# A hybrid attention and gated-layer kernel: the third token tile loaded and transposed earlier, around the value projections of the first tiles

## The chip, the cores and the metric

The kernel runs on one core of one Trainium2 chip. The metric is the device time of one execution in microseconds (us). The five engines of the core run side by side and meet at semaphores: PE (TensorE: matmuls and transposes; its weight loads are shown as PEld), DVE (VectorE), ACT (ScalarE), POOL (GpSimd) and SP (SyncE, which issues the DMAs).

## What is computed

`x` has 2048 tokens of 512 numbers, in bf16. It is normalised once and goes through two branches whose results are added to it:

```
xn  = layernorm(x)
qkv = xn @ wqkv                                  # 32 heads of 16
phi_q, phi_k = softmax(+-(q @ w_phi)), softmax(+-(k @ w_phi))   # joined, 32 features
kv, z = sum over tokens of phi_k * v, of phi_k
o   = (phi_q @ kv) / (phi_q . z + 1e-6)
out = x + o @ wo + ((xn @ w_gate) * (xn @ w_up)) @ w_down       # 1792 hidden columns
```

## The kernel before

The 2048 tokens are 16 tiles of 128 rows. A tile must be layer-normed and transposed (`xnT`, the contraction dimension on the partitions) before PE can multiply it with a weight. For tiles 4 to 15 this runs beside PE's other work, and DMA does the transposing. For tiles 0 to 3, at the start, it is done on the spot, and this is the part that the change touches:

- `centre(n)` (lines 174 to 180): on DVE, the statistics of tile n (`bn_stats` at L156, `bn_aggr` at L157) and the subtraction of the mean (L177, gives `xn`); then two small POOL instructions (L161, L162) that give the row scale `rst`.
- `lt(n)` (lines 213 to 222): PE transposes the four 128-column blocks of `xn` into one PSUM bank (L219), and ACT copies them to `xnT` in two halves (L222).
- `proj(ps, n, wv, js)` (L251): up to four matmuls of 512 columns, the value projection v of tile n, one for each 128-row block j of `wv`. Block j needs the j-th part of `xnT` of that tile, and the half of `wv` that holds it: blocks 0 and 1 lie in the first half, 2 and 3 in the second.
- `vcopy(n, ps, eng)` (lines 338 to 345): v, scaled by `rst`, from PSUM to SBUF, on ACT (L343) or DVE (L345).
- `half(w, ...)` (L285): four matmuls that make one 128-column block of gate or up, here for the first 256 tokens only (tiles 0 and 1); `gate_copy` (L291, ACT) and `hidden` (L297, DVE) take it out of PSUM.

The schedule is written by hand (`manual_schedule`): each engine executes its instructions in the order in which the program text issues them, and an instruction that waits holds up all that follow it on its engine. So the lines 349 to 377 are the order of each of the engines at the start. Before the real work PE runs nine matmuls on constants (`warm_up`, L334), whose result is not used.

All loads are issued by SP on one queue, in the order of lines 84 to 101. The sixteen DMA engines share out each load. A DMA's landing here means that all its parts have arrived.

PSUM has eight banks. In the first part two of them hold `pv[0]` and `pv[1]`; the other six (`bank()`) go round: each new tile takes the bank that was given out six calls earlier, and waits for that one's last reader.

After these lines the program is one long row of gate and up matmuls, k, v and q projections, sums over tokens, and in the end the output projections (`fin`, L315 and L318).

Of the kernel before, what the change touches and what calls it, by code (L numbers as in the profile page):

```python
# [21 lines left out]
def kernel(  # L22
# [12 lines left out]
    nc = tc.nc  # L35
# [6 lines left out]
    DC = D // P  # L42
# [21 lines left out]
    wv = wpool.tile([P, DC, D], BF16)  # L64
# [9 lines left out]
    def dma_x(lo, hi):  # L74
        nc.sync.dma_start(out=xall[:, lo:hi, :], in_=x_view(lo, hi))

    def dma_cols(eng, w, src, lo, hi, at=0):
        eng.dma_start(out=w[:, :, lo - at:hi - at], in_=src[:, lo:hi].rearrange("(c p) f -> p c f", p=P))
# [7 lines left out]
    for lo in (0, 2):  # L86
        nc.sync.dma_start(out=wv[:, lo:lo + 2, :],
                          in_=A_wqkv[lo * P:(lo + 2) * P, 2 * D:3 * D].rearrange("(c p) f -> p c f", p=P))
    dma_x(2, 3)
    dma_cols(nc.sync, wg, B_w_gate, 0, 2 * P)  # L90
    dma_x(3, 4)
    dma_cols(nc.sync, wu, B_w_up, 0, 2 * P)
# [56 lines left out]
    def bank(name, dt=F32, n=TT):  # L149
        return ps_s.tile([P, n], dt, name=name, tag="s")  # L150
# [3 lines left out]
    def ln_stats(n, mv):  # L154
        stats = lnpool.tile([P, nc.vector.BN_STATS_DIM], F32, name="stats")
        nc.vector.bn_stats(out=stats[:], in_=xall[:, n, :])  # L156
        nc.vector.bn_aggr(out=mv, in_=stats[:])  # L157

    def ln_rstd(mv, k, rstd):
        ve = lnpool.tile([P, GT], F32, name="ve")  # L160
        nc.gpsimd.tensor_scalar(out=ve[:, 0:k], in0=mv[:, 0:k, 1], scalar1=EPS, scalar2=None, op0=ALU.add)  # L161
        nc.gpsimd.tensor_tensor(out=rstd, in0=ve[:, 0:k], in1=mhalf[:, 0:k], op=ALU.pow)  # L162
# [11 lines left out]
    def centre(n):  # L174
        ln_stats(n, mv0[:, n, :])
        xn = xnpool.tile([P, D], BF16, name="xn")
        nc.vector.tensor_scalar(out=xn[:], in0=xall[:, n, :], scalar1=mv0[:, n, 0:1], scalar2=None,  # L177
                                op0=ALU.subtract)
        ln_rstd(mv0[:, n:n + 1, :], 1, rst[:, n:n + 1])
        xns[n] = xn  # L180
# [32 lines left out]
    def lt(n, nbanks=1):  # L213
        step = DC // nbanks
        tps = []
        for lo in range(0, DC, step):
            tp = bank("tp", BF16).rearrange("p (c t) -> p c t", c=DC)
            for c in range(lo, lo + step):
                nc.tensor.transpose(out=tp[:, c, :], in_=xns[n][:, c * P:(c + 1) * P], identity=ident[:])  # L219
            tps.append(tp)  # L220
        for lo in range(0, DC, 2):
            nc.scalar.copy(out=xnT[:, lo:lo + 2, n * P:(n + 1) * P], in_=tps[lo // step][:, lo:lo + 2, :])  # L222
# [3 lines left out]
    def make_bd():  # L226
        bo, wp = BO[:], wphi[:]
        nc.vector.tensor_tensor(out=bd[:], in0=_bcast_ap(bo, [bo.ap[0], [0, DC], [E1, 8], [1, DH]]),
                                in1=_bcast_ap(wp, [wp.ap[0], [DH, DC], [0, 8], [1, DH]]), op=ALU.mult)
# [19 lines left out]
    def proj(ps, n, w, js=range(DC)):  # L249
        for j in js:  # L250
            nc.tensor.matmul(ps, lhsT=xnT[:, j, n * P:(n + 1) * P], rhs=w[:, j, :],  # L251
                             start=(j == 0), stop=(j == DC - 1))
# [29 lines left out]
    def half(w, name, T, f, lo, hi):  # L282
        ps = bank(name)[:, 0:hi - lo]
        for c in range(DC):
            nc.tensor.matmul(ps, lhsT=w[:, c, f * P:(f + 1) * P], rhs=xnT[:, c, T * TT + lo:T * TT + hi],  # L285
                             start=(c == 0), stop=(c == DC - 1))
        return ps

    def gate_copy(ps, n):
        g_sb = gpool.tile([P, TT], BF16, name="g_sb")  # L290
        nc.scalar.copy(out=g_sb[:, 0:n], in_=ps)  # L291
        return g_sb

    def hidden(T, f, ps, g_sb, lo, hi):
        if T not in hTs:
            hTs[T] = hpool.tile([P, FC, TT], BF16, name="hT", tag="h")
        nc.vector.tensor_tensor(out=hTs[T][:, f, lo:hi], in0=ps, in1=g_sb[:, 0:hi - lo], op=ALU.mult)  # L297
# [34 lines left out]
    def warm_up(k, n=TT):  # L332
        for _ in range(k):
            nc.tensor.matmul(warm[:, 0:n], lhsT=ones[:, 0:P], rhs=ones[:, 0:n], start=True, stop=True)  # L334
# [3 lines left out]
    def vcopy(n, ps, eng=nc.scalar):  # L338
        dst, src = vts[n % NV][:, :, :, 0:DH], ps.rearrange("p (a b c) -> p a b c", a=8, b=4)
        if n >= GT:  # L340
            nc.scalar.copy(out=dst, in_=src)  # L341
        elif eng is nc.scalar:
            nc.scalar.activation(out=dst, in_=src, func=AF.Identity, scale=rst[:, n:n + 1])  # L343
        else:
            eng.tensor_scalar(out=dst, in0=src, scalar1=rst[:, n:n + 1], scalar2=None, op0=ALU.mult)  # L345

    with tc.tile_pool(name="ps_v", bufs=1, space=PSUM) as ps_v:
        pv = [ps_v.tile([P, D], F32, name=f"pv{n}") for n in range(2)]
        centre(0)
        centre(1)  # L350
        lt(0, nbanks=2)
        warm_up(1)
        proj(pv[0][:], 0, wv, range(1))
        lt(1)
        proj(pv[0][:], 0, wv, range(1, DC))
        proj(pv[1][:], 1, wv)
        centre(2)
        vcopy(0, pv[0])
        lt(2)
        g = [half(wg, "g", 0, f, 0, 2 * P) for f in range(2)]  # L360
        g_sb = [gate_copy(ps, 2 * P) for ps in g]
        centre(3)
        vcopy(1, pv[1], nc.vector)
        pv2 = bank("pv")
        proj(pv2, 2, wv, range(2))
        lt(3)
        proj(pv2, 2, wv, range(2, DC))
        vcopy(2, pv2, nc.vector)
        for f in range(2):
            hidden(0, f, half(wu, "u", 0, f, 0, 2 * P), g_sb[f], 0, 2 * P)  # L370
        pv3 = bank("pv")
        proj(pv3, 3, wv)
        vcopy(3, pv3, nc.vector)
        make_bd()
        nc.gpsimd.tensor_scalar(out=nrst[:], in0=rst[:], scalar1=-1.0, scalar2=None, op0=ALU.mult)
        nc.gpsimd.tensor_tensor(out=r2[:], in0=rst[:], in1=rst[:], op=ALU.mult)
        nc.gpsimd.tensor_tensor(out=M4[:], in0=BO[:, 0:4, :], in1=BO[:, 4:8, :], op=ALU.add)
# [138 lines left out]
```

## Time and profile before

| | us |
|---|---|
| median of three runs | 221.6 (221.21 to 221.74) |
| the profiled execution: its time | 221.94 |
| the profiled execution: its span | 220.2 |
| PE busy in the span | 214.7 (97%) |
| DVE busy | 140.3 (64%) |
| ACT busy | 87.5 (40%) |
| POOL busy | 73.0 (33%) |

The span is what the profile shows from the first instruction to the last; 1.7 us of the execution's time lie around it. The granted TensorE clock is shown as 1.00. Matmuls are pipelined: the duration of one runs on into the next, so the step from one start to the next is what a matmul costs PE. A row "0.59 ... x2" with 379 ns for one says that the second started 0.21 us after the first.

### The profile page before, as it was taken

The page shows a single profiled execution, that of the slowest core. Times are in us where ns is not written, and L with a number is a line of the kernel's source. Part 1 is how long each engine was busy: PE and PEld are TensorE (multiplying, and loading weights), DVE is VectorE, ACT ScalarE, POOL GpSimd, SP SyncE. Part 2 cuts the span into 40 slices and gives each one's busy share as a digit, 9 for nine tenths or more (in the row PEclk, how much of TensorE's full clock was granted, in tenths as well). Part 3 has the DMA queues.
Part 4 walks back from the last instruction along what each step waited for, and adds up shares of the span by engine and source line. Part 5 has one row for each costly group of instructions (what it writes and reads, how often), then busy time and mean ns, then how long its engine had stood idle before and what let it go on. Part 6 is the DMA issues. An engine that isn't in the chain of part 4 may idle for free.

```text
span 220.2 us, 3493 instructions
## 1 busy us (share of the span) xinstructions
PE 214.7 (97%) x1283; PEld 104.8 (48%) x1307; DVE 140.3 (64%) x239; ACT 87.5 (40%) x161; POOL 73.0 (33%) x64
## 2 busy tenths in 40 slices
PE   8999999999999999999999999999999999999994
PEld 3564445444444444444454444444444444454443
DVE  5667976886598766657499874197655745454321
ACT  3525587458654775464444221231322322100000
POOL 5500556363338573635135433033033033000000
PEclk9999999999999999999999999999999999999999
DMA  6999995402202241202008345214431431412401
GB/s 186 235 310 385 367 224 75 87 0 51 48 0 48 51 72 25 48 3 46 4 18 130 71 95 116 55 24 95 95 74 24 95 71 28 93 50 71 72 26 48
DMA packets 47249, 19.91 MB, mean 90 GB/s; under 512 B 37504, under 2 KB 46976, under 8 KB 47104
## 3 DMA queue, kind: packets, MB, share of 16 engines
q1 hardware_dynamic: 47232, 19.69, 37.8%
q8 instruction: 10, 0.16, 0.3%
q14 instruction: 7, 0.06, 0.1%
HBM read 8.67 MB, written 2.10 MB: 49 GB/s over the span
## 4 chain that ended last, share of the span: by engine, by line
PE 88%; DVE 3%; DMA 2%; issue 2%; ACT 1%; POOL 1%; SPq 1%; DVEq 0%; ACTq 0%
PE fin L315 22%; PE g L285 20%; PE u L285 20%; PE fin L318 6%; PE q L251 6%; PE k L251 5%; PE pv L251 5%; DMA xall<-in_A_x_dram 2%; PE ab L458 2%; PE kv L397 2%; DVE sums L266 1%; DVE stats L156 1%; ACT e L262 1%; DVE rs L268 1%; POOL rstd L162 0%
## 5 line engine op out<-in xcount | busy, mean ns | idle before, releaser
L285 PE MATMUL g<-xnT,wg 128*128 128x512 bf16 (+1 forms) x227 | 57.2, 371 | 0.4
L285 PE MATMUL u<-xnT,wu 128*128 128x512 bf16 (+1 forms) x231 | 57.5, 372 | 0.1
L297 DVE TENSOR_TENSOR hT<-u,g_sb 128x512 bf16<-128x512 f32 (+1 forms) x58 | 37.1, 648 | 24.2 <-PE u L285 15.4
L291 ACT CAST g_sb<-g 128x512 bf16<-128x512 f32 (+1 forms) x58 | 33.3, 575 | 48.2 <-PE g L285 48.1
L266 DVE TENSOR_REDUCE sums<-e 128x64 f32<-128x1024 f32 x32 | 38.9, 1216 | 20.5 <-ACT e L262 20.5
L270 POOL TENSOR_TENSOR phiq<-e,rs 128x1024 bf16<-128x1024 f32 x16 | 30.9, 1933 | 62.9 <-DVE rs L268 54.1
L315 PE MATMUL fin<-wd,hT 128*128 128x512 bf16 (+2 forms) x231 | 50.3, 366 | 0.3
L270 POOL TENSOR_TENSOR phik<-e,rs 128x1024 bf16<-128x1024 f32 x16 | 30.9, 1932 | 44.5 <-DVE rs L268 32.3
L285 PEld LDWEIGHTS <-wu 128*128 128x128 bf16 x232 | 22.7, 98 | 25.9
L315 PEld LDWEIGHTS <-hT 128*128 128x128 bf16 x238 | 22.5, 98 | 24.7
L285 PEld LDWEIGHTS <-wg 128*128 128x128 bf16 x232 | 22.0, 98 | 23.4
L251 PEld LDWEIGHTS <-xnT 128*128 128x128 bf16 x192 | 17.5, 98 | 17.8 <-ACT xnT L222 0.6
L251 PE MATMUL pv<-wv,xnT 128*128 128x512 bf16 x62 | 22.1, 386 | 0.2
L326 DVE TENSOR_TENSOR o_sb<-fin,xall 128x512 bf16<-128x512 f32 (+2 forms) x13 | 8.4, 650 | 20.5 <-PE fin L318 19.7
L251 PE MATMUL k<-W1k,xnT 128*128 128x512 bf16 x61 | 20.7, 379 | 0.0
L268 DVE RECIPROCAL rs<-sums 128x64 f32<-128x64 f32 x32 | 17.7, 553 | 3.1
L318 PE MATMUL fin<-wo,oT 128*128 128x512 bf16 (+2 forms) x66 | 16.3, 366 | 0.1
L251 PE MATMUL q<-W1q,xnT 128*128 128x512 bf16 x60 | 16.0, 378 | 0.2
L260 ACT ACTIVATE e<-q 128x512 f32<-128x512 f32 x12 | 7.2, 597 | 22.2 <-PE q L251 22.2
L341 ACT CAST vt<-pv 128x512 bf16<-128x512 f32 x12 | 7.0, 587 | 16.9 <-PE pv L251 16.9
L156 DVE BATCH_NORM_STATS2 stats<-xall 128x6 f32<-128x512 bf16 x16 | 10.7, 670 | 3.0 <-DMA xall<-in_A_x_dram 2.9
L468 DVE TENSOR_TENSOR otok<-ab,rden 128x512 bf16<-128x512 f32 x16 | 11.1, 691 | 0.6
(55 smaller groups left out, 126.4 us busy)
## 6 DMA issues: line engine op xcount, KB each, us to landing
out_dram<-o_sb SPq DMA_DIRECT2D x15, 128.0 KB, 1.9
wd<-in_B_w_down_dram SPq DMA_DIRECT2D x1, 1792.0 KB, 15.5
wg<-in_B_w_gate_dram SPq DMA_DIRECT2D x2, 640.0 KB, 6.8
wu<-in_B_w_up_dram SPq DMA_DIRECT2D x2, 640.0 KB, 8.0
xall<-in_A_x_dram SPq DMA_DIRECT2D x1, 1024.0 KB, 11.9
xall<-in_A_x_dram SPq DMA_DIRECT2D x4, 128.0 KB, 3.2
wv<-in_A_wqkv_dram SPq DMA_DIRECT2D x2, 256.0 KB, 2.9
wg<-in_B_w_gate_dram SPq DMA_DIRECT2D x2, 256.0 KB, 4.8
```

The costliest lines, as they stand in the source:

```text
L156: nc.vector.bn_stats(out=stats[:], in_=xall[:, n, :])
L251: nc.tensor.matmul(ps, lhsT=xnT[:, j, n * P:(n + 1) * P], rhs=w[:, j, :], start=(j == 0), stop=(j == DC - 1))
L266: nc.vector.tensor_reduce(out=sums[:], in_=ev, axis=AX.X, op=ALU.add)
L268: nc.vector.reciprocal(out=rs[:].rearrange("p a b -> p (a b)"), in_=sums[:])
L270: nc.gpsimd.tensor_tensor(out=phi[:].rearrange("p g (x f) -> p (g x) f", f=DH), in0=ev, in1=rs[:].to_broadcast((P, 2 * H, DH)), op=ALU.mult)
L285: nc.tensor.matmul(ps, lhsT=w[:, c, f * P:(f + 1) * P], rhs=xnT[:, c, T * TT + lo:T * TT + hi], start=(c == 0), stop=(c == DC - 1))
L291: nc.scalar.copy(out=g_sb[:, 0:n], in_=ps)
L297: nc.vector.tensor_tensor(out=hTs[T][:, f, lo:hi], in0=ps, in1=g_sb[:, 0:hi - lo], op=ALU.mult)
L315: nc.tensor.matmul(ps, lhsT=hTs[T][:, f, t4 * P:(t4 + 1) * P], rhs=wd[:, f, lo:lo + w], start=(f == 0), stop=False)
L318: nc.tensor.matmul(ps, lhsT=oTs[n][:, c, :], rhs=wo[:, c, lo:lo + w], start=False, stop=(c == DC - 1))
L326: nc.vector.tensor_tensor(out=o_sb[:], in0=ps, in1=xres, op=ALU.add)
L468: nc.vector.tensor_tensor(out=o_tok[:].rearrange("p (b h d) -> p b h d", b=2, d=DH), in0=abv[:, :, :, 0:DH], in1=rden[:].to_broadcast((P, ...
```

## The change

The load of x tile 2 is issued between the two halves of `wv` instead of behind both. On PE, the transposes of tile 2 go between the second and third matmul of v of tile 1, all of v of tile 2 goes ahead of the two gate blocks, and the transposes of tile 3 go behind these blocks, in one piece with nothing of v around them. On DVE, `centre(2)` has its old place behind `centre(1)`, and one `vcopy` less is to be done: that of tile 1 goes to ACT. On ACT, the copies of `xnT` of tile 2 now precede the two `vcopy`s. No instruction is added or removed, except that v of tile 1 is scaled by an ACT instruction in place of a DVE one.

```
     for lo in (0, 2):
         nc.sync.dma_start(out=wv[:, lo:lo + 2, :],
                           in_=A_wqkv[lo * P:(lo + 2) * P, 2 * D:3 * D].rearrange("(c p) f -> p c f", p=P))
-    dma_x(2, 3)
+        if lo == 0:
+            dma_x(2, 3)
     dma_cols(nc.sync, wg, B_w_gate, 0, 2 * P)
...
         proj(pv[0][:], 0, wv, range(1, DC))
-        proj(pv[1][:], 1, wv)
         centre(2)
+        proj(pv[1][:], 1, wv, range(2))
+        lt(2)
+        proj(pv[1][:], 1, wv, range(2, DC))
         vcopy(0, pv[0])
-        lt(2)
+        vcopy(1, pv[1])
+        pv2 = bank("pv")
+        proj(pv2, 2, wv)
         g = [half(wg, "g", 0, f, 0, 2 * P) for f in range(2)]
         g_sb = [gate_copy(ps, 2 * P) for ps in g]
         centre(3)
-        vcopy(1, pv[1], nc.vector)
-        pv2 = bank("pv")
-        proj(pv2, 2, wv, range(2))
+        vcopy(2, pv2, nc.vector)
         lt(3)
-        proj(pv2, 2, wv, range(2, DC))
-        vcopy(2, pv2, nc.vector)
         for f in range(2):
             hidden(0, f, half(wu, "u", 0, f, 0, 2 * P), g_sb[f], 0, 2 * P)
         pv3 = bank("pv")
```

## The prediction

> **What bounds the kernel now.** I read the page first: PE is busy for 97% of the span and makes up 88% of the chain that ended last. Then PE's own waits, over the whole span:
>
> ```profile
> PE 214.7 (97%) x1283; PEld 104.8 (48%) x1307; DVE 140.3 (64%) x239; ACT 87.5 (40%) x161; POOL 73.0 (33%) x64
> PE 88%; DVE 3%; DMA 2%; issue 2%; ACT 1%; POOL 1%; SPq 1%; DVEq 0%; ACTq 0%
> ```
>
> ```profile
> PE warm L334 <- PEq L500: 0.8, 1, 0.8
> PE tp L219 <- DVE xn L177: 0.5, 1, 0.5
> ```
>
> Besides the start PE waits just once, in the first slices, for `xn` of tile 2. Behind that, its starts follow one another at the pace of the matmuls up to the end at 217 us. So what is won or lost on PE before about 12 us arrives at the end in full, unless another engine or a load is late by then. The chain of waits says what the one wait hangs on (start, length):
>
> ```profile
> 2.69 4.27 DMA xall<-in_A_x_dram
> 6.96 0.02 issue
> 6.98 0.70 DVE stats L156
> 7.71 0.19 DVE mv L157
> 7.90 0.02 issue
> 7.93 0.36 DVE xn L177
> 8.29 0.05 issue
> 8.34 0.40 PE tp L219 x4
> ```
>
> Tile 2 of x, issued at 2.69, lands at 6.96; DVE needs 1.31 (6.98 to 8.29), and the transposes start at 8.34. PE's timeline gives the size of the wait (start, length, in brackets the idle time):
>
> ```profile
> 5.50 0.63 PE L219 MATMUL tp<-ident,xn 128*128 128x128 bf16 x4
> 5.93 1.86 PE L251 MATMUL pv<-wv,xnT 128*128 128x512 bf16 x7
> 8.34 0.40 PE L219 MATMUL tp<-ident,xn 128*128 128x128 bf16 x4 [0.55 <-DVE xn L177]
> 8.57 1.04 PE L285 MATMUL g<-xnT,wg 128*128 128x256 bf16 x8
> ...
> 11.62 0.81 PE L251 MATMUL pv<-wv,xnT 128*128 128x512 bf16 x3
> 12.27 0.60 PE L285 MATMUL g<-xnT,wg 128*128 128x256 bf16 x4
> ```
>
> The last v matmul of tile 1 starts at 7.41 (narrow window) and costs 0.216, the step between starts, so PE could go on at 7.63. The wait is 8.34 - 7.63 = 0.71; the bracket's 0.55 counts from the modelled end. The start of the g matmuls behind v of tile 3, 12.27, is my yardstick.
>
> **Loads.** SP issues x2 at 2.18 in place of 2.69 and the second half of wv at about 2.7 in place of 2.18, each in about 0.47; all later issues keep their times. The first half of wv lands at 4.47, the second at 5.25, so 256 KB took 0.78 and a tile of x (128 KB) about 0.39. x2 then lands at 4.47 + 0.39 = 4.86 and wv's second half at 5.25 + 0.39 = 5.64. These are estimates from landings. For the other end: before, x2 landed 1.71 behind wv, not 0.39. The packet records show one 1 KB packet, begun at 5.19, of 1.34 us, where most took some 0.05; fifteen of x2's sixteen parts had landed by 5.85, the last at 6.96. Nothing says whether this packet belongs to that place in the queue, to that moment, or to this one execution.
>
> **DVE, tile 2.** DVE is free at 5.39 (`centre(1)` ends 5.04 + 0.35) and x2 is there. `centre(2)` ends at 5.40 + 1.31 = 6.71, and its transposes may start at 6.76. Its two POOL instructions move forward with it; no other work is queued there.
>
> **PE, step by step.** Up to 6.98 the order is as before: v of tile 0 needs wv's second half at 6.33 (landing 5.64), and matmuls 0 and 1 of tile 1 start at 6.76 and 6.98. Transposes at 7.195, 0.44 behind the 6.76 that they need; four at 0.056 (0.40 less 0.22 for one, over three), to 7.42. Matmuls 2 and 3 of tile 1, to 7.85. Putting transposes into an open sum I cost at nothing else: tile 1's stood so in v of tile 0, and the next row starts 0.11 behind the last of them.
>
> Now v of tile 2, which has no gate work left between it and its own transposes. Last transpose at 7.36, its length 0.22, 0.04 to ACT, the copy 0.37, 0.06 to the weight load and matmul (the steps from tile 1's rows: 5.82, 6.18, 6.55, 6.60): 8.05. PE is free at 7.85, so a **new wait** of 0.20. ACT is idle then: `vcopy(0)` now stands behind the copies. The second copy ends at 8.27, before matmul 2 needs it at 8.48. Bounds: nothing, if the copy starts half done, to 0.43, if the 0.86 from tile 0's transposes to its first v (4.24 to 5.10, matmuls still at double the step) holds, less the cover of two matmuls; the row that it is nearest to is tile 1's, so 0.20.
>
> Four matmuls to 8.91. Gates: eight at 0.109, to 9.79; `wg` landed at 7.97, so no wait. Transposes of tile 3: `xn` was ready for them at 9.75 (PEld row), DVE's order up to there is unchanged, x3 lands where it did: 9.79 to 10.01. Up: to 10.88 (`wu` landed at 9.23). v of tile 3 needs the copy of its transposes: last one at 9.95 + 0.22 + 0.04 = 10.21; ACT has by then `vcopy(0)` 8.16, `vcopy(1)` 8.74 (0.58 a step, as two 512-wide ACT rows at 20.94 and 21.52), gate copies at 9.55 and 9.99, so the copy runs from about 10.26 to 10.63, ready at 10.68, under cover of the up matmuls by 0.2. Four matmuls: yardstick at **11.75 in place of 12.27: -0.52**, that is the 0.71 gone and the 0.20 new.
>
> Edits at nothing, with their cover: `vcopy(2)` on DVE (0.75) starts behind `centre(3)` at 9.61, ends at 10.36; v of tile 3 takes that bank, the sixth later, at 10.88: 0.5 of cover. `vcopy(1)` on ACT is read by the sums at 31 us. Later loads: wu's third part lands at 17.28 and was used at 19.01; now at 18.5. Transposed tile 4 landed at 32.91 behind the last weight loads and was used at 34.36; now at 33.8, 0.9 of cover. So the gain is not given back by a load.
>
> **The sum.** 221.94 - 0.52 = 221.42, made against the profiled execution's own time, which is 0.34 above the median of 221.6. I don't subtract that 0.34 again: if part of the 0.71 was absent in the other runs, it is the very thing that made them shorter, and without it before would be 221.94 - 0.71 = 221.23, close to the lowest run, 221.21. Forecast **221.4**, that is no change that a measurement of this kernel (about 0.3%, 0.66 us) can tell.
>
> The page "TensorE: Matmul & The Clock Gate" of the Trainium skill (Part 1) says that the clock doubles at the end of a free-running window of about 3.4 us, so at another moment in each execution. Here the 512-column steps go from 0.43 to 0.22 at 6.3, while the clock is shown as 1.00 throughout. By that rule an earlier doubling would let PE reach the wait sooner: both kernels' times then spread by several tenths, in the direction of a larger gain.
>
> **Rivals.**
>
> *The tile is not late in most runs.* If x2 lands by 5.85, as fifteen of its parts did, `xn` is ready at 5.87 + 1.36 = 7.23, ahead of 7.63: before has no wait, and after still has its 0.20. For: runs 0.2 to 0.7 below the profiled one, one slow packet. Against: the profile is what there is. Time: 221.6 + 0.2 = 221.8.
>
> *The late part falls on wv (slower).* The second half of wv now stands last of the pair, with less slack: needed at 6.33, estimated 5.64. If the slow packet stays at its moment or place, that half lands at 6.96 as the pair did, and v of tile 0 waits 0.63 at its third matmul, with everything behind it. Then 221.42 + 0.63 = 222.05, slower than before by 0.1 of its profiled time and 0.45 of the median. It loses against the profiled time from a landing at 6.85 on, and by over 0.3% of the median from 7.17 on. Against: wv's halves landed in 2.8 and 3.1 us, without a laggard. The page "DMA: Bandwidth & Descriptors" of the Trainium skill ("Why a DMA increments its semaphore by 16 and not by 1") speaks for this rival: a wait ends only when the slowest of the engines has delivered. Hanging on it: x2's parts, from 5.40 to 6.96, agree.
>
> *More is won.* If PE runs ahead of the profiled pace, before waits longer for the same late tile, and the new order gains up to the whole wait and some: 221.94 - 0.71 and the profile's own 0.34 less give 220.9. For: the wait ends by a load, at a fixed time. Against: the 0.20 needs a copy that is not faster then.
>
> *The change does nothing,* because the wait moves whole to v of tile 2 or to tile 3's transposes, which have 0.04 to spare: 221.6. It takes an `xn` of tile 3 later by 0.5, which only a later x3 makes; its issue has not moved.
>
> **Chances.** Forecast 0.45, tile not late 0.2, late wv 0.15, more won 0.15, nothing 0.05. Faster by over 0.3% (below 220.94): two thirds of "more won" and a little of the forecast, 0.18. Slower by over 0.3% (above 222.26): half of "late wv", some of "tile not late", and what I haven't seen, 0.17. Within: 0.65. Range 220.85 (more won) to 222.15 (late wv).
>
> **What would show it.** Right: x2 landed near 4.9, `stats` of tile 2 at 5.4, transposes in the v row of tile 1 at 7.2, no wait for `xn`, an idle weight load of about 0.2 until ACT's copy ahead of v of tile 2, g of tiles 2 and 3 near 11.75. Wrong: a PE wait at the third v matmul of tile 0 that ends by wv, a wait ahead of tile 3's transposes, or a PE wait behind 12 us that was not there.

## The result, and the profile after

| | us |
|---|---|
| before, median of 20 runs | 221.68 (221.05 to 222.29) |
| changed, median of 20 runs | 222.03 (221.66 to 222.49) |
| ratio | 1.0017, 95% interval 1.0009 to 1.0025 |
| profiled execution after: time, span | 222.22, 220.5 |

The change costs 0.35 us. It was forecast to bring 0.2 to 0.5, so the direction was wrong; the time lies in the range, and near the 222.05 that the rival "the late part falls on wv" had worked out. That the median meets this number to 0.02 is partly luck: the rival's sum starts from a profiled execution, and the one profiled after the change took 222.22, 0.17 more than the sum (0.07 from the start of the waiting matmul, 7.03 in place of 6.96, and 0.10 from a later place, see below). PE's waits in the changed kernel (us in total, times, longest):

```profile
PE pv L252 <- DMA wv<-in_A_wqkv_dram: 0.9, 1, 0.9
PE warm L335 <- PEq L501: 0.8, 1, 0.8
PE pq L239 <- ACT g_sb L292: 0.2, 1, 0.2
```

The wait for `xn` of tile 2 is gone, and one for the second half of `wv` is there, longer than the old one. The third line, a short wait of a projection fold at 51 us, is new too. The chain of waits names the same load, in the place where x tile 2 stood before (2.69, 4.27):

```profile
2.69 4.30 DMA wv<-in_A_wqkv_dram
6.98 0.04 issue
7.03 1.02 PE pv L252 x4
```

PE's timeline after:

```profile
5.77 0.38 PE L252 MATMUL pv<-wv,xnT 128*128 128x512 bf16 x1
7.03 1.02 PE L252 MATMUL pv<-wv,xnT 128*128 128x512 bf16 x4 [0.88 <-DMA wv<-in_A_wqkv_dram]
7.89 0.39 PE L220 MATMUL tp<-ident,xn 128*128 128x128 bf16 x4
8.11 1.66 PE L252 MATMUL pv<-wv,xnT 128*128 128x512 bf16 x6
...
11.58 1.03 PE L252 MATMUL pv<-wv,xnT 128*128 128x512 bf16 x3
12.45 0.38 PE L286 MATMUL g<-xnT,wg 128*128 128x256 bf16 x2
```

The second v matmul of tile 0 frees PE at 5.99, the third starts at 7.03: 1.04 lost (the bracket's 0.88 counts from the modelled end). Everything behind runs as the prediction stepped it, 5.42 from the third matmul to the yardstick (6.33 to 11.75 in the sum), and the yardstick is 12.45 in place of 12.27. That is 0.18 of the 0.28 between the two profiled executions. The other 0.10 arises at 41.8 us, see below.

The stages from 4 to 6 us, first before, then after (the last column is GB/s moved by the DMA engines, the one ahead of it their busy share):

```profile
4.00:5.00 1.00, 1.00 (x6) 0.45 (x5) 0.96 (x3) 0.33 (x2) 0.86 (x2) 1.00 1.05 350
5.00:6.00 1.00, 1.00 (x7) 0.66 (x7) 0.35 (x2) 0.32 (x2) 0.82 (x2) 1.00 1.05 265
```

```profile
4.00:5.00 1.00, 1.00 (x6) 0.45 (x5) 0.96 (x3) 0.27 (x2) 0.91 (x2) 1.00 0.96 201
5.00:6.00 1.00, 1.00 (x7) 0.47 (x7) 0.96 (x3) 0.40 (x3) 0.77 (x2) 1.00 0.71 215
```

From 4 to 5 us the DMA engines were about as busy (0.96 against 1.05) but moved far less; from 5 to 6 us they were less busy too (0.71). The packet records say how: eight 1 KB packets that began between 4.50 and 4.71 took 0.57 to 0.81 us each, where most take about 0.05.

### The profile page after: what moved, and what is told of

It reads as the page before. It is cut to its first block, busy times and chain, and to the rows that moved or that the text cites. A ratio compares the mean times of both kernels' runs of the same rounds, so it can differ in the third digit from the quotient of the medians.

```text
span 220.5 us, 3492 instructions
## 1 busy us (share of the span) xinstructions
PE 214.5 (97%) x1283; PEld 104.5 (47%) x1307; DVE 139.7 (63%) x238; ACT 88.1 (40%) x162; POOL 73.0 (33%) x64
## 4 chain that ended last, share of the span: by engine, by line
PE 89%; DVE 3%; DMA 2%; issue 2%; ACT 1%; POOL 1%; SPq 1%; DVEq 0%; ACTq 0%
PE fin L316 22%; PE g L286 20%; PE u L286 20%; PE fin L319 6%; PE q L252 6%; PE pv L252 6%; PE k L252 5%; DMA wv<-in_A_wqkv_dram 2%; PE ab L459 2%; PE kv L398 2%; DVE sums L267 1%; ACT e L263 1%; SPq L75 1%; DVE stats L157 1%; DVE rs L269 1%
```

## The experiments

My theory, "late load": of the five loads that PE needs first, the last lands near 7 us whichever it is, and the change puts the one last that is needed first. Rivals: "engine order" (the new order on PE costs the time, the loads are a gain) and "one-off" (the late x tile 2 was peculiar to one execution). Ratios are against before, run beside it on the same chip, with 95% intervals; medians in us. Each trace is of one execution.

### One part at a time

**e1, the load order alone** (in the kernel before):

```
-    dma_x(2, 3)
+        if lo == 0:
+            dma_x(2, 3)
```

> The kernel before with the change's load order alone (x tile 2 between the halves of wv), the order on the engines as before. Theory 'late load' (whichever load stands fifth lands near 7.0 us, before x tile 2 at 6.96, after the change wv's second half at 6.98): PE waits at the third v matmul of tile 0 until about 7.03; six matmuls of 0.216 end at 8.32, where tile 2's transposes started before anyway (8.34). So the time is that of before, ratio 0.999 to 1.001. Rival 'engine order' (the loss of the change comes from the new order on PE, and the load order is a gain): tile 2 is no longer waited for, about 0.5 to 0.7 us less, ratio 0.997.

Measured: 0.9995 (0.9985 to 1.0006), 221.53 against 221.75. No gain, as "late load" says. PE's timeline in e1:

```profile
7.23 1.45 PE L252 MATMUL pv<-wv,xnT 128*128 128x512 bf16 x6 [0.86 <-DMA wv<-in_A_wqkv_dram]
8.52 0.39 PE L220 MATMUL tp<-ident,xn 128*128 128x128 bf16 x4
```

The half lands at 7.18 and tile 2's transposes start 1.34 later, behind six matmuls of 0.216; before, x tile 2 landed at 6.96 and they started 1.38 later, behind DVE's three instructions. In the old order the two loads weigh the same, so swapping them is worth nothing. (This profile is of the slowest of e1's twelve executions, 222.12.)

**e2, the order on the engines alone** (the changed kernel with `dma_x(2, 3)` behind both halves).

> The changed order on the engines with the load order of before (x tile 2 behind both halves of wv). Theory 'late load': x tile 2 lands near 6.96 again, its transposes wait in the middle of v of tile 1 until 8.34, two v matmuls and the 0.2 us wait for the copied transposes stand behind them: 8.34 + 0.17 + 0.68 = 9.19 for v of tile 2, and gate of tiles 2 and 3 starts near 12.9 in place of 12.27 (before) and 12.45 (the change): 222.2 to 222.4, ratio 1.003. Rival 'one-off' (the late x tile 2 was peculiar to the profiled execution and most executions have none): only the 0.2 us are added, 221.9, ratio 1.001.

Measured: 1.0009 (0.9997 to 1.0020), 221.81. The runs fall in two groups: eight at 221.58 to 221.83, four at 222.37 to 222.51. The four are near where "late load" put them all (222.2 to 222.4). The profiled execution is one of the eight, and x tile 2 landed at 6.05 in it; the other eleven left no trace. So "one-off" had a part: with the loads in the order of before, x tile 2 is not late in every execution.

**e3, the wait for wv taken away:**

```
-        proj(pv[0][:], 0, wv, range(1, DC))
+        proj(pv[0][:], 0, wv, range(1, DC), blocks=2)     # rhs = w[:, j % blocks, :]
```

> The changed kernel, where v of tile 0 takes the blocks of wv's first half twice, so that PE doesn't wait for the second half there; everything else is as in the change, and tile 0's v is thereby another product. Theory 'late load': the 0.9 to 1.0 us wait at the third v matmul goes; gate of tiles 2 and 3 starts at 11.6 to 11.75 in place of 12.45, and the time is 0.5 to 0.9 us below that of the change: 221.2 to 221.5, ratio 0.998. Rival 'engine order': the wait is cover for something else that is late (x tile 3, or gate weights) and the time stays within 0.2 us of the change, ratio 1.001 to 1.002.

Measured: 0.9986 (0.9976 to 0.9996), 221.52. That is 0.5 us below the changed kernel's 222.03, or 0.7 by the two ratios, and 0.2 to 0.3 us below before: without the wait the new order is a gain of about the size forecast. e3's profile is of the slowest of its twelve executions, 221.88, and has the yardstick at 12.12, beyond the expected 11.75; the median, less the 209.76 that pass behind the yardstick there, puts it at 11.76.

**e5, the changed kernel again:**

> The changed kernel itself, on the same chip as the next three. By its first runs (ratio 1.0017) it should stand at 1.001 to 1.0025. Theory 'late load' says that its profile again shows the load of wv's second half landing at 6.5 to 7.2 and PE's one wait ending by it, and few GB/s at 4 to 6 us (201 and 215 in its first profile, 350 and 265 before); theory 'one-off' says that the landing scatters and is near 5.6 in some executions, as this one may be.

Measured: 1.0031 (1.0015 to 1.0048), 222.21 against 221.71, with one execution of the twelve at 224.06 (see the last section); the half landed at 7.02, and 274 and 135 GB/s were moved at 4 to 6 us. Not a one-off.

**e10, what was late next before.** The prediction read 221.23 for a kernel before without tile 2's wait.

```
-        lt(2)
+        lt(2, src=1)          # transposes xns[1]
```

> The kernel before, where the transposes of tile 2 read the centred tile 1, so that PE doesn't wait for x tile 2; tile 2 thereby has tile 1's values in its place. Theory 'tile 3 is late next': the transposes of tile 3 stood 0.13 us behind their input in the profile before (9.88 against 9.75), so taking away tile 2's wait uncovers tile 3's: they start at 9.4 to 9.8, the gate of tiles 2 and 3 at 11.8 to 12.2 in place of 12.27, 221.5 to 221.9, ratio 0.999 to 1.000. The prediction's reading (without tile 2's wait before would take 0.71 less): 221.0 to 221.2, ratio 0.997.

Measured: 1.0000 (0.9986 to 1.0014), 221.71 against 221.59. Taking tile 2's wait away wins nothing: tile 3 is late behind it. PE's weight loads for tile 3's transposes, before and in e10:

```profile
9.75 0.34 PEld L219 LDWEIGHTS <-xn 128*128 128x128 bf16 x4 [0.21 <-DVE xn L177]
```

```profile
8.96 0.23 PEld L219 LDWEIGHTS <-xn 128*128 128x128 bf16 x4 [0.47 <-DVE xn L177]
```

Both wait for `xn`. In e10's profile x tile 3 landed early (7.58), and that execution took 221.06. Four of its twelve runs are of that kind, 220.94 to 221.23, where the prediction's reading had them all; the other eight took 221.57 to 221.98, which by the same steps (3.79 from the landing of x tile 3 to the yardstick, 209.69 from there to the time) is a landing at 8.1 to 8.5, where other profiles have it (8.37 before, 8.24 after). That x tile 3 was late in these eight is worked out, not seen: none of them was profiled.

### Using the late half later

**e7** (in the changed kernel):

```
-        proj(pv[0][:], 0, wv, range(1, DC))
+        proj(pv[0][:], 0, wv, range(1, 2))
         centre(2)
         proj(pv[1][:], 1, wv, range(2))
         lt(2)
+        proj(pv[0][:], 0, wv, range(2, DC))
         proj(pv[1][:], 1, wv, range(2, DC))
```

> The changed kernel where PE takes the four matmuls on wv's second half of tiles 0 and 1 behind the transposes of tile 2, in place of ahead of them and around them. The second half is needed at about 7.1 in place of 6.0 to 6.3, and four matmuls (0.86 us) cover the copy of tile 2's transposes. Theory 'late load': both waits go, and a wait of at most 0.4 for the copied transposes of tile 1 is left; gate of tiles 2 and 3 at 11.6 to 11.9 in place of 12.45: 221.3 to 221.6, ratio 0.998 to 0.9995. If the load was not what cost the time, the ratio stays at 1.001 to 1.002.

Measured: 0.9996 (0.9985 to 1.0007), 221.58, against 222.21 for the changed kernel (e5) on the same chip. PE's timeline in e7:

```profile
6.04 1.28 PE L252 MATMUL pv<-wv,xnT 128*128 128x512 bf16 x3
7.15 0.39 PE L220 MATMUL tp<-ident,xn 128*128 128x128 bf16 x4
7.37 1.89 PE L252 MATMUL pv<-wv,xnT 128*128 128x512 bf16 x8
```

The half landed at 7.19, later than in the changed kernel, and nothing waits: it is first used at 7.37, and eight v matmuls run through, tile 2's among them, whose copy is now covered.

**e4, e6, e12, e9, e11: x tiles 1 and 2 in one load ahead of wv** (`dma_x(1, 3)` in place of two), under the changed order (e4), the old order (e6, and e12 the same again), e7's order (e9), and e7's with v of tile 1 scaled on DVE (e11).

> The changed kernel with x tiles 1 and 2 in one load of 256 KB, ahead of wv: x tile 2 no longer has an issue of its own, and wv's second half is the fourth load in place of the fifth, with the same bytes ahead of it. Theory 'late load' by place in the queue: the second half lands by 5.9, the wait of PE goes, and the fifth load, the gate weights, takes the lateness where it is not needed until 8.9: ratio 0.997 to 0.998, 221.1 to 221.3. The same theory by moment or bytes (what moves between 4.5 and 7 us is held up): the second half lands near 7.0 as in the change, ratio 1.001 to 1.002. Rival 'engine order': ratio 1.001 to 1.002 with the second half landed early.

> The order on the engines of before, with x tiles 1 and 2 in one load of 256 KB ahead of wv. Theory 'late load': x tile 2 lands by 3.9 and is not waited for; if wv's second half lands by 6.4, as in the same loads under the changed order (6.43), tile 2's transposes start when PE is free, near 7.6, and gate of tiles 2 and 3 near 11.6 to 11.9: 221.2 to 221.5, ratio 0.998; where that half lands near 7.0, as before, ratio 1.000. Theory 'engine order' (the new order is worth its place once the loads are mended): not below e4 with the same loads, ratio 1.000 or above.

> e6 once more (the order of before with x tiles 1 and 2 in one load), beside e9 on the same chip: 0.9993 with its interval of 0.9979 to 1.0008 before; theory 'late load' expects 0.998 to 0.9995, and the same time as e9 to within 0.2 us.

> The order on PE of e7 (second half of wv used behind the transposes of tile 2) with the loads of e4 and e6 (x tiles 1 and 2 in one load). Theory 'late load': nothing that lands late is needed before it lands, so only the wait for the copied transposes of tile 1 (up to 0.4) is left: gate of tiles 2 and 3 at 11.5 to 11.9, 221.2 to 221.6, ratio 0.998 to 0.9995. If joined loads had not mended anything, it would be as e4, 1.0005.

> e9 with v of tile 1 scaled on DVE, behind v of tile 3, in place of ACT. From the gate of tiles 2 and 3 to the last matmul the changed kernel took 205.00 us and the kernel before 204.90, in every profile so far; the 0.10 arises at 41.8 us on ACT. If it comes with the one ACT instruction more, this run shows 204.90 and 0.1 us less than e9, ratio 0.0004 lower; if it comes from another place in the new order, 205.00 and the ratio of e9.

| | ratio | median | wv's second half landed |
|---|---|---|---|
| e4 | 1.0005 (0.9990 to 1.0019) | 221.77 | 6.43 |
| e6 | 0.9993 (0.9979 to 1.0008) | 221.37 | 6.54 |
| e12 | 1.0013 (0.9998 to 1.0029) | 221.86 | 7.14 |
| e9 | 0.9994 (0.9982 to 1.0005) | 221.41 | 7.17 |
| e11 | 0.9992 (0.9980 to 1.0003) | 221.45 | 7.33 |

As the fourth load the half landed 0.4 to 0.6 earlier than the 6.98 of the changed kernel in two profiles and no earlier in three, so it isn't the fifth place alone. e6 and e12 are one kernel: in its two profiled executions the time follows the landing (221.38 and 221.98). e12 and e9 ran on one chip with the same loads and the same landing; PE's waits in e12 show what e9 doesn't have:

```profile
PE pv L250 <- DMA wv<-in_A_wqkv_dram: 1.1, 1, 1.1
```

That is the lesson of e7 once more, though e12 and e9 differ in their whole order at the start: 0.45 between the medians. e7 against the changed kernel, and e9 against e4, are the cleaner pairs: there only two matmuls move, those of tile 0 on the second half, as tile 1's two stand behind the transposes of tile 2 already. Two expectations were missed here: e4 fits neither the early half nor the late one, and e12 is not within 0.2 us of e9. e9 and e11 are below the change (their intervals end at 1.0005 and 1.0003, its own begins at 1.0009). Their intervals reach 1, so it isn't shown that they beat the kernel before, or e1 and e7.

### Why the load is late

**e8, x tile 2 third, ahead of both halves; e13, 128 KB of `wo` between the halves (in the kernel before); e14, gate weights behind x tile 3; e15, the 16 KB of `w_phi` third (in the kernel before).**

> The changed kernel with x tile 2 loaded third, ahead of both halves of wv, so that nothing stands between these; wv's second half is still the fifth load. If it is the place in the queue, or the moment, that is late, the half lands near 7.0 and the ratio is that of the change, 1.001 to 1.0025. If it is the x tile between two halves of wv that slows the moving of data (201 and 215 GB/s at 4 to 6 us in the changed kernel's profile), the rate is back near 300 or over, the half lands by 6.2, and the ratio is 0.998 to 1.000. Against both: wv's first half lands 0.4 us later, near 4.9, just ahead of its first use at 5.1.

> The kernel before with 128 KB of another tensor (the first 128 rows of wo) loaded between the halves of wv, where the change puts x tile 2; x tile 2 stays behind them. In three profiles with wv's halves third and fourth the second half landed at 5.25 to 5.96, in nine with x tile 2 ahead of it at 6.4 to 7.3. If it is the moment or the bytes ahead (a transfer that begins near 4.4 us is held up), the half lands at 6.4 to 7.3 here too. If it is x tile 2 that is read ahead, it lands one such load later than before, 5.6 to 6.2. Time 221.9 to 222.4, since x tile 2 comes later.

> The changed kernel with the first gate weights, whose packets are 512 B, loaded behind x tile 3 in place of ahead of it. If these packets, on engines that have done their part of wv, are what holds up the others, wv's second half lands by 6.2 and the ratio is 0.998 to 1.000. If not, it lands at 6.4 to 7.3 as in the change, the ratio stays at 1.001 to 1.003, and x tile 3 lands 0.4 earlier for nothing.

> The kernel before with the 16 KB load of w_phi issued third, ahead of wv: every load behind it is issued about half a microsecond later, with hardly any bytes more ahead. If it is the moment (what is under way from about 4.4 us on is held up), wv's second half, begun half a microsecond later, lands at 6.4 or later; if it is the bytes or the x tile ahead, at 5.7 to 6.4. The time can rise by as much as wv is later, to 222.5, since its first half is used at 5.1.

**e16, e17, e18: the second half of wv issued from ACT's queue**, in e9 at the start, in the changed kernel and in e7 behind ACT's first activation in the program.

> e9 (joined x tiles, second half of wv used late) with the second half of wv issued from ACT's queue at the start, beside x tile 0 from SP's. The half then lands long before it is used (by 5.0), and the first x tiles, which share the DMA engines with it, up to 0.4 later than 2.9 and 3.9. If a late second half is all that is left, the time is that of e9 or up to 0.2 below it, 221.2 to 221.5; if x tile 0, which all of PE's first work hangs on, comes later by 0.3, the time is 0.1 to 0.3 above e9: 221.5 to 221.8.

> The changed kernel with wv's second half issued from ACT's queue behind ACT's first activation, at about 2.3 us, so that it shares the DMA engines with wv's first half and x tile 2 but not with x tile 0. With a part of wv on ACT's queue all five first loads had landed by 5.9 in the run before this (e16), against 6.4 to 7.3 on one queue. If that holds here the half lands by 6.2, PE waits at most 0.2 for it, and the time is 221.3 to 221.6, ratio 0.998 to 1.000. If wv's first half, which shares with it, lands behind its use at 5.1 by more than 0.4, the start is later by that and the ratio stays above 1.001.

> The same loads as e17 under the order of e7, where PE uses wv's second half behind the transposes of tile 2. If the half lands by 6.2, this order has nothing more to hide and is 0 to 0.2 us beside e17; with a late first half both lose the same.

First loads in the order in which they were issued (w0, w1 the halves of wv), landing of w0, w1 and x2, GB/s from 4 to 5 us:

| | order | w0 | w1 | x2 | GB/s | ratio |
|---|---|---|---|---|---|---|
| before | x0 x1 w0 w1 x2 | 4.47 | 5.25 | 6.96 | 350 | |
| e2 | x0 x1 w0 w1 x2 | 4.91 | 5.64 | 6.05 | 355 | 1.0009 |
| e15 | x0 x1 w_phi w0 w1 x2 | 5.07 | 5.80 | 6.95 | 367 | 222.0, one run |
| changed | x0 x1 w0 x2 w1 | 4.57 | 6.98 | 4.90 | 201 | 1.0017 |
| e14 | x0 x1 w0 x2 w1, x3 next | 4.83 | 6.87 | 5.30 | 225 | 1.0017 (1.0008 to 1.0026) |
| e13 | x0 x1 w0 wo w1 x2 | 4.73 | 6.92 | 7.33 | 289 | 222.37, one run |
| e8 | x0 x1 x2 w0 w1 | 5.99 | 7.26 | 4.07 | 237 | 1.0007 (0.9987 to 1.0026) |
| e16 | x0 x1+x2 w0; w1 on ACT | 5.88 | 4.37 | 5.13 | 368 | 1.0043 (1.0016 to 1.0069) |
| e17 | x0 x1 w0 x2; w1 on ACT | 5.17 | 4.09 | 5.64 | 277 | 1.0015 (1.0004 to 1.0026) |
| e18 | x0 x1 w0 x2; w1 on ACT | 6.77 | 3.92 | 7.14 | 234 | 1.0035 (1.0012 to 1.0058) |

x tile 2 is not the culprit (e13: another tensor in its place, the half at 6.92), nor are the 512 B packets behind (e14), nor a fifth place (e15: the fifth landed at 5.80, the sixth at 6.95). e15's half was issued 0.54 later than before (2.72 against 2.18) and was still on time, so the moment of issue alone isn't it either; the bytes ahead remain a rival that no run tests by itself. e13 and e15 are one run each. On SP's queue the last of x0, x1, x2, w0, w1 landed at 6.05 to 7.33 in all seventeen profiles, mostly near 7. It wasn't quite the same whichever was last: with the loads in the order of before (before, e2, e10) x tile 2 landed at 6.96, 6.05 and 6.37, with those of the change (after, e1, e3, e5, e7, e14) wv's half at 6.87 to 7.19.

The second queue gets w1 in by 4.4 and delays x tile 0 instead, the tile that everything starts from: 3.46 and 3.37 in e16 and e17, against 2.86 before. (e17's profile is of an execution of 221.56, 0.5 below its median.) And in e18 the lateness fell on w0 and x tile 2. e8's median, 221.63, is below the 222.21 of the change on the same chip all the same; its one trace is of an execution of 223.67 us and can't tell why. The ratios of e16 and e18 contain three executions each of 223.8 to 224.2 us (last section); their medians, 222.22 and 222.16, stand 0.44 and 0.38 above before.

Expectations missed: e16 and e17, which I had at or below before; in e17 and e18 the half was issued at 0.84, not at 2.3 as I had expected, so the load was not kept clear of x tile 0.

What holds up the packets that begin between 4.3 and 5.6 us stays open: no recorded instruction fetch lies there. Packets of over 0.3 us begin earlier too, between 1.8 and 4.3 us, in nineteen of the twenty profiles; and the profiles of e2 and e16 have none between 4.3 and 5.6.

## Why the prediction was wrong

- **x tile 2, DVE, the transposes: right.** Landing 4.90 (4.86 forecast), statistics at 5.36 (5.40), `xn` at 6.65 (6.71).
- **"wv's second half at 5.25 + 0.39 = 5.64": wrong, the step that failed.** It landed at 6.98. I took the pace of an undisturbed stretch and added to it, and left the 1.3 us of x tile 2's lateness with x tile 2. e1 and e5 (7.18 and 7.02) show the half late in its new place again, and e13 (6.92) that it is so behind another tensor. The rival had the mechanism and the 6.96; I gave it 0.15 on the ground that wv's halves "landed in 2.8 and 3.1 us, without a laggard", which held of their old place alone. Its wait of 0.63 came out as 1.04, as PE was free at 5.99, not at 6.33 (the traces carry a record of the clock, which has it doubled at 5.53, against 6.29 before); the wait's end is the landing, so that did not change the time.
- **The new wait of 0.20 behind tile 2's transposes: right**, 8.54 to 8.74 in the profile, where PE's weight load waits for ACT's copy:

```profile
8.73 0.11 PEld L252 LDWEIGHTS <-xnT 128*128 128x128 bf16 x2 [0.52 <-ACT xnT L223]
```

  Its upper bound of 0.43 was mis-worked: 0.86 from the first transpose at 7.195 is 8.055, which is 0.20 behind 7.85; the transposes' own 0.22 was left out. The loads win nothing (e1), and this wait remains.
- **"Without it before would be 221.94 - 0.71 = 221.23": wrong.** In the median, none of the 0.71 was to be had in the old order (four of e10's twelve executions had it). Tile 3's `xn` was ready at 9.75 for transposes at 9.88, which I used as cover for the new order and didn't apply to the old one. e10 shows that taking the wait away leaves the median where it was, and its trace that PE's weight load then waits for tile 3's `xn`. The rival "the tile is not late in most runs" leaned on the same sum.
- **Behind the yardstick nothing was to change: 0.10 off.** From the yardstick to the last matmul 205.00 us pass after and 204.90 before. One ACT instruction starts 0.58 behind its predecessor in place of 0.48, and the chain of ACT, DVE and POOL that the fold at 51 us waits for is later by that. Before, and after:

```profile
41.34 0.59 ACT L341 CAST vt<-pv 128x512 bf16<-128x512 f32 x1 [1.79 <-PE pv L251]
41.82 0.60 ACT L260 ACTIVATE e<-k 128x512 f32<-128x512 f32 x1
```

```profile
41.52 0.59 ACT L342 CAST vt<-pv 128x512 bf16<-128x512 f32 x1 [1.79 <-PE pv L252]
42.10 0.60 ACT L261 ACTIVATE e<-k 128x512 f32<-128x512 f32 x1
```

  It is there in seven of eight profiles with the change's order on the engines, and in none with the old order or e7's. It isn't the one ACT instruction more, since e7 and e9 have that too, so that e11's question had fallen away. In both traces the events that the later instruction waits for stand at the same distance from the yardstick, so no later input is seen. Why is open.

So the account: -0.1 from the loads (e1), about +0.2 from the order with its new wait and the 0.10 (e2), neither told from nothing by its interval, and the rest because the two meet: the order with the late half in front of it. The ratios alone would not tell these parts from one another; the wait in the trace does, and e3 and e7, which take it away and are 0.5 to 0.6 below the change.

## What to carry to other kernels

When loads on one queue are permuted, let the landing of the last one stay at least where it was, whatever is put there, and ask what its new owner is needed for; a pace from two undisturbed landings is no forecast. What helps is the order of use: matmuls on the part that lands last moved behind work that has its data (e7, e9). And before a wait is counted as gain, look at which input is ready just ahead of its use behind it.

## What the runs showed of the hardware

A pause of PE near the start can go with a loss far larger than itself. In e18's profile PE waited for w0 from 5.2 to 6.8, behind a pause of 0.55 up to 4.58. The stages (clock third from the end):

```profile
6.00:7.00 1.00, 0.19 (x1) 0.10 (x1) 0.00 (x0) 0.00 (x0) 0.47 (x1) 0.97 1.08 329
7.00:8.00 1.00, 1.00 (x6) 0.47 (x4) 0.80 (x2) 0.23 (x1) 0.00 (x0) 0.50 1.08 270
...
9.00:10.00 1.00, 1.00 (x7) 0.70 (x6) 0.64 (x3) 0.30 (x2) 0.69 (x3) 0.50 1.00 249
10.00:11.00 1.00, 1.00 (x6) 0.37 (x5) 0.00 (x0) 0.74 (x3) 0.91 (x4) 0.83 1.15 163
```

The granted clock falls to half at 6.93 and comes back at 10.35. That execution took 224.16, two us above the median of its kernel, and two more of its eleven runs took 223.93 and 224.14. In e18's clock record the clock had doubled at 3.52, so the three steps lie 3.41 and 3.42 us apart. The page "TensorE: Matmul & The Clock Gate" of the Trainium skill (Part 1) puts the fall behind an idle window of about 3.4 us; the length of the half-clock stretch agrees with that window, but here the pauses of 0.55 and 1.61 us within the window ahead of the fall went with it, and PE was not idle throughout.

In e8's profile PE stood still for 0.7 (5.36 to 6.03) with the clock not yet doubled. The doubling came at 10.12 there, in place of 3.5 to 6.7 by the clock records of the other traces that have one, and the execution took 223.67. e7's came at 6.70, without such a pause, and e8's is 3.42 behind that.

Three of e16's ten runs took 223.80 to 223.92, and one run of the changed kernel (e5) 224.06, all at a mean granted clock of 0.992, which is what 3.42 us at half clock make of 222 us. None of these was profiled, so that their clock fell for a pause is likely, not shown.
